# Banded attention with a feed-forward layer, one core: the attention values of twelve pairs move to another PSUM bank and to another place in TensorE's queue

## The chip, the cores and the metric

The kernel runs on one core of a Trainium2 chip. The metric is the time of one execution in device microseconds (us). Before the change, three runs gave 850.41, 850.63 and 853.78 us; the median is 850.63 us.

## What is computed

Queries, keys and values for 8 batches, 8 heads, 576 positions and 64 channels go through attention with a band of 64 positions. The result, 4608 rows of 512, goes through two matrix products with a leaky ReLU between them.

```python
scores = scale * np.matmul(q, k.transpose(0, 1, 3, 2))
mask = (rel >= 0) & (rel < window)          # rel = query - key position, window = 64
attn = softmax of the masked scores
out = np.matmul(attn, v)
x = out as 4608 x 512
h = x @ w_in                                # 512 x 2048
g = np.maximum(0.01 * h, h)
return g @ w_out                            # 2048 x 512
```

## The kernel before

**Attention in pairs.** A block is 64 queries of one batch and all 8 heads. There are 72 blocks, taken two at a time as 36 *pairs* m. For a pair, TensorE writes the scores into two PSUM banks, "s" and "t" (32 matmuls of 64x64 for each bank, 64 in all, L278). VectorE adds the mask (E, L677), GpSimd takes the maximum (P) and the sum (A), VectorE subtracts the maximum (B, L699), ScalarE takes the exponential (X, L703), and TensorE multiplies with the values (V, `values_of`, L751: 32 matmuls that read 128 rows and write 64 columns). ScalarE then copies the values out of PSUM (`take_of`, L758, called the *take* here), and VectorE multiplies them by the reciprocals of the sums (Y, L763).

**The feed-forward layer** comes in stages. Rows 0 to 1535 (pairs 0 to 11, three chunks c of 512 rows) are computed directly. Its first layer makes a unit of 128 channels, `h_f`, in one PSUM bank out of 12 matmuls of 128x512 (`early_first`, L938, two calls of 6 each); its second layer adds each unit to four accumulators, `acc_0` to `acc_3`, with 4 times 3 matmuls (`early_second`, L947). Each factor is held as a high and a low part, hence three products per term. The list `walk` sets which unit follows which: first layer of unit n, then second layer of unit n-2, and so on, 24 matmuls a step. The units' banks alternate between "o" and "h". The unit's eviction is a chain: ScalarE applies the leak in the bank (L952), ScalarE copies the high part to one of two buffers (`gs`, L955; it waits until the second layer of two units before has read that buffer), VectorE makes the low part (L958). The bank is free after that.

All of this runs beside attention for pairs 8 to 19, called *early* in the code (`EARLY = 20`), between about 139 and 309 us of the span. The three later chunk groups use products of a recursive block scheme (m, L1136; y, L1156; z, L1199); pairs 20 to 35 run beside those. The first of them needs the outputs of pairs 12 to 19 as rows of x, by way of DRAM (`x_build`, L912 and L915).

**Where an early pair's values go.** `values_of` takes bank "t" for pairs 8 to 19, one of the two banks of the scores. So a pair's values have to wait until the scores of a pair ahead have been read out of "t", and the scores after that wait for the take.

**What sets the order.** Up to 139 us the order is written out by hand. From there on `op(...)` records each piece of work with its engine, an estimated duration and what it comes after, and `arrange` makes one order for each engine: at every step it takes the piece that can begin first, and of those that can begin then the one with the lowest rank. [...] `next_main` chains the feed-forward matmuls, so these keep their own order and the pieces of attention fall between them. DMAs are issued from ScalarE's (ACT) and SyncE's (SP) queues and, for the stream of weights, from GpSimd's (POOL).

Of the kernel before, what the change touches and what calls it, by code (L numbers as in the profile page):

```python
# [37 lines left out]
PAIRED = 8  # L38
# [5 lines left out]
LAG = 2.0  # L44
ROOMS = 3
OWN = 4
TAKEN = 4
# [57 lines left out]
def band_attention_ffn(ctx: ExitStack, tc: tile.TileContext, qk, vW, vL, w_in, w_out, eye_mask, out, outT):  # L105
# [16 lines left out]

    of_h, of_a = cycle("oh"), cycle("st")

# [300 lines left out]
    def mm1(c, f, part):  # L425

        xh, xl = xs[c]
        ps = bank(next(of_h) if c or f >= half else "h", f"h{c}_{f}_{part.start}")[:, part]
        wh, wl = wi[f]
        terms = [(a, b, k) for k in range(KT) for a, b in ((wh, xh), (wh, xl), (wl, xh))]  # L430
        for n, (a, b, k) in enumerate(terms):
            nc.tensor.matmul(ps, a[:, k, :], b[:, k, part], start=n == 0, stop=n == len(terms) - 1)  # L432
        t = []

        def leak():
            t.append(temps[:, :CH][:, part])
            nc.scalar.activation(t[0], ps, AF.Prelu, alpha=0.01)

        def high():
            t2 = pairs_of_g[next(turns) % 2]  # L440
# [91 lines left out]

    def op(engine, us, fn, *after, rank=1.0, lag=0.12, land=0.0):
        x = dict(engine=engine, us=us, fn=fn, after=[a for a in after if a], rank=rank, lag=lag, land=land, n=len(plan))
        plan.append(x)
# [9 lines left out]
    def arrange():  # L545
# [3 lines left out]
        for x in plan:  # L549
# [3 lines left out]
            if not x["after"]:  # L553
                waiting[x["engine"]].append((0.0, x))
        order, landed = [], [0.0] * LANES

# [3 lines left out]
        while any(waiting.values()):  # L560
# [6 lines left out]
            t, e = best  # L567
            r, x = min((y for y in waiting[e] if begins(*y) <= t), key=lambda y: (y[1]["rank"], y[1]["n"]))
            waiting[e] = [y for y in waiting[e] if y[1] is not x]
# [57 lines left out]

    def next_main(us, fn, *after):
        nonlocal main
        main = op("PE", us, fn, *after, main)  # L630
        return main
# [112 lines left out]
    def values_of(m):  # L744
        ps = bank("t" if early(m) else "oh"[m % 2], f"o{m}")
        for w in range(UNITS):
# [35 lines left out]
    def attend(m, gate):  # L782
# [8 lines left out]
        if m > PAIRED:  # L791
            o["v"] = bulk(partial(load_v, m, nc.scalar), before["X1"], rank=0.3 + late, lag=1.0 + 2 * late, land=6.5 + 2 * late)
        takes = [before["take"], two["take"]] if m == EARLY else []
        if held_back(m - 1) and before:
            takes += [before["B0"], before["B1"]]
        held = held_back(m)
        takes += [before.get("E0"), before.get("E1"), three.get("take"), s_free]
        masks = [op("ACT", ACTS, partial(mask_to, m, j), *takes, rank=0.4 + late) for j in range(2)] if held else takes
        urge = [before["X0"], before["X1"]] if m > EARLY and m % 2 == 0 else []
        o["S"] = op(  # L800
            "PE", 1.0, partial(scores_of, m), o.get("k"), *masks, *urge, before.get("S"),
            rank=0.5 + late, lag=LAG if early(m) else 2 * LAG,
        )
# [19 lines left out]
    def normalise(m):  # L823

        late = 0.0 if early(m) else 0.45
        soon = 0.15 if early(m) and m > 13 else 0.8 + late
        o, before, two, after = at[m], at.get(m - 1, {}), at.get(m - 2, {}), at.get(min(m + 2, EARLY - 1))
# [15 lines left out]
    def finish_of(m, spread, late, soon):  # L843
        o, before, two, after = at[m], at.get(m - 1, {}), at.get(m - 2, {}), at.get(min(m + 2, EARLY - 1))
        mate, ahead = at.get(m ^ 1, {}), at.get(m + 2, {})
        if early(m):
            free = [after["E1"], before.get("take"), o["A0"] if direct(m) else o["I"]]
        else:
            free = [both_free if early(m - 2) else two["Y"]]
            free += [] if m % 2 else [mate["X0"], mate["X1"], ahead.get("S")]  # L850
        o["V"] = op("PE", 1.0, partial(values_of, m), o.get("v"), o["X0"], o["X1"], *free, before.get("V"), rank=0.5 + late, lag=LAG if early(m) else 2 * LAG)
        kept = two.get("kept", [])
        if early(m):
            o["take"] = op("ACT", ACTS, partial(take_of, m), o["V"], *kept, rank=0.5 + late)
        o["Y"] = op("DVE", TWO if early(m) else ONE, partial(product_of, m), *spread, o.get("take"), o["V"], *kept, rank=soon, lag=0.3 + 6 * late)
# [72 lines left out]
    def early_first(n, part):  # L928
        c, f = walk[n]
        xh, xl = xs[c]  # L930
        if part == 0:
            h_of[n] = bank(next(of_h), f"h{c}_{f}")
        ps = h_of[n]
# [45 lines left out]
    def second_step(n):  # L979
        c, f = walk[n]  # L980
        free = evicted[c - 1] if n in opens else [None] * 4
        seconds[n] = [next_main(3 * MM, partial(early_second, n, i), lows[n], free[i], *ready[f]) for i in range(4)]
        if c == 2:
# [8 lines left out]
    for n, (c, f) in enumerate(walk):  # L992
        next_main(6 * MM, partial(early_first, n, 0), lows.get(n - 2), *ready[f], *(x2 if c == 2 else ()))
        first = next_main(6 * MM, partial(early_first, n, 1))
        if n == 0:
# [449 lines left out]
```

## Time and profile before

| | before |
|---|---|
| median of 3 runs | 850.63 us |
| the profiled execution: whole time / its span | 849.76 us / 847.9 us |
| TensorE busy, DVE busy, ACT busy, POOL busy | 839.7, 604.3, 390.1, 383.4 us |
| granted TensorE clock | 1.00 |
| DMA | 226.79 MB, mean 267 GB/s |
| values of the early pairs (L751), first and last take (L758) | 12 takes, 173.9 to 308.9 us |

The profile is one execution of the program. PE is TensorE's matmul row, DVE is VectorE, ACT is ScalarE, POOL is GpSimd. A line of the timeline reads: start, duration, engine, source line, operation, tile written <- tiles read, shape, count, and in square brackets how long the engine stood idle before it and for what. Matmuls overlap, so the duration of a group is not its price; the distance from its start to the next group's start is.

### The profile page before, as it was taken

To read this page: it belongs to the slowest core of one execution; us is meant where nothing else is said; L and a number is where in the kernel's file an instruction comes from. 1 tells how busy PE (TensorE), PEld (TensorE's weight loads), DVE (VectorE), ACT (ScalarE), POOL (GpSimd) and SP (SyncE) were. 2 spreads that over 40 slices of the span, in tenths; PEclk is the share of its full clock that TensorE was granted. 3 is DMA by queue.
4 is the path that set the end of the run, shared out by engine and by line. 5 is a ranking of instruction groups with operands and counts; after the bars stand their busy time and mean duration, and the time that the engine had idled before them with its cause. 6 is when DMAs were issued, how large, how long until landed. Compare 5 with 4: busy or idle time off the path is not lost.

```text
span 847.9 us, 16820 instructions
## 1 busy us (share of the span) xinstructions
PE 839.7 (99%) x6778; PEld 685.6 (81%) x6778; DVE 604.3 (71%) x851; ACT 390.1 (46%) x637; POOL 383.4 (45%) x218
## 2 busy tenths in 40 slices
PE   8999999999999999999999999999999999999998
PEld 5787888888878888888888888888888888888886
DVE  6999885748768778656669956475679855446863
ACT  4666654333433355554554544543354533324431
POOL 5322000878888716776777767855111111111110
PEclk9999999999999999999999999999999999999999
DMA  9874756898899969999999999999998886677682
GB/s 330 268 235 152 252 163 235 265 283 282 272 316 313 318 208 287 303 319 340 334 336 354 361 344 315 363 315 302 260 268 234 236 247 196 199 199 198 193 215 89
DMA packets 143116, 226.79 MB, mean 267 GB/s; under 512 B 15552, under 2 KB 66880, under 8 KB 143040
## 3 DMA queue, kind: packets, MB, share of 16 engines
q0 software_dynamic: 51552, 90.18, 38.3%
q10 hardware_dynamic: 51024, 77.31, 28.5%
q1 hardware_dynamic: 40464, 58.24, 21.1%
q8 instruction: 53, 0.87, 0.4%
q14 instruction: 23, 0.19, 0.1%
HBM read 172.52 MB, written 53.06 MB: 266 GB/s over the span
## 4 chain that ended last, share of the span: by engine, by line
PE 88%; DMA 5%; DVE 5%; ACT 1%; issue 1%; ACTq 0%; SPq 0%; DVEq 0%
PE m L1136 27%; PE z L1199 18%; PE acc L947 11%; PE h L938 11%; PE y L1156 5%; PE h L432 4%; PE acc L468 4%; PE s L278 4%; PE o L751 3%; DMA more_v<-vL 2%; DMA raw<-w_out 1%; DMA late_r<-rows 1%; DMA rows<-late_c 1%; DVE w L242 1%; PE o L368 1%
## 5 line engine op out<-in xcount | busy, mean ns | idle before, releaser
L1136 PE MATMUL m<-pfew,p 128*128 128x512 f32 x720 | 168.7, 390 | 0.0
L1136 PEld LDWEIGHTS m<-pfew,p 128*128 128x128 f32 x720 | 134.6, 188 | 28.3
L1120 POOL DMA_DIRECT2D p<-w_first x42 | 31.7, 755 | 109.0 <-PE m L1136 67.5
L947 PE MATMUL acc<-p,gs 128*128 128x512 f32 x324 | 80.4, 394 | 0.0
L1145 DVE TENSOR_TENSOR p<-m,pxa 128x512 f32<-128x512 f32 x60 | 41.4, 690 | 50.7 <-PE m L1136 48.3
L1145 DVE TENSOR_TENSOR pxa<-m,pxa 128x512 f32<-128x512 f32 x60 | 41.3, 689 | 46.3 <-PE m L1136 45.8
L695 POOL PARTITION_ALL_REDUCE late_o<-late_f x20 | 65.6, 3306 | 16.4 <-ACT late_f L703 9.4
L1148 ACT ACTIVATE p<-p 128x512 f32<-128x512 f32 x60 | 37.8, 631 | 76.3 <-DVE p L1145 76.2
L692 POOL PARTITION_ALL_REDUCE g<-late_f x20 | 36.8, 1872 | 78.7 <-DVE late_f L677 71.3
L1136 PE MATMUL m<-pxb,p 128*128 128x512 f32 x288 | 70.4, 390 | 0.0
L947 PEld LDWEIGHTS acc<-p,gs 128*128 128x128 f32 x324 | 59.9, 188 | 12.8
L695 POOL PARTITION_ALL_REDUCE late_o<-e x18 | 59.8, 3339 | 17.9 <-issue 8.3
L695 POOL PARTITION_ALL_REDUCE late_o<-late_e x18 | 60.1, 3358 | 15.4 <-issue 9.5
L1136 PEld LDWEIGHTS m<-pxb,p 128*128 128x128 f32 x288 | 53.8, 188 | 11.3
L1199 PE MATMUL z<-gs,p 128*128 128x512 f32 x240 | 57.6, 389 | 0.0
L938 PE MATMUL h<-pxa,p 128*128 128x512 f32 x228 | 55.2, 391 | 0.0
L1199 PEld LDWEIGHTS z<-gs,p 128*128 128x128 f32 x240 | 45.0, 188 | 9.4
L1199 PE MATMUL z<-third,p 128*128 128x512 f32 x216 | 51.9, 389 | 0.0
L1199 PE MATMUL z<-pxa,p 128*128 128x512 f32 x216 | 51.9, 389 | 0.0
L1120 POOL DMA_DIRECT2D p<-w_second x28 | 22.7, 811 | 63.9 <-PE z L1199 37.0
L938 PEld LDWEIGHTS h<-pxa,p 128*128 128x128 f32 x228 | 42.6, 188 | 9.0
L1199 PEld LDWEIGHTS z<-third,p 128*128 128x128 f32 x216 | 40.5, 188 | 8.4
(193 smaller groups left out, 1744.4 us busy)
## 6 DMA issues: line engine op xcount, KB each, us to landing
p<-w_first POOLq DMA_DIRECT2D x42, 1024.0 KB, 7.1
p<-w_second POOLq DMA_DIRECT2D x28, 1024.0 KB, 7.7
p<-w_sums POOLq DMA_DIRECT2D x16, 1024.0 KB, 5.6
qk<-qk ACTq DMA_DIRECT2D x26, 512.0 KB, 6.6
pspare<-w_second ACTq DMA_DIRECT2D x16, 512.0 KB, 7.9
w_sums<-pspare ACTq DMA_DIRECT2D x16, 512.0 KB, 7.6
raw<-w_out ACTq DMA_DIRECT2D x15, 512.0 KB, 4.2
raw<-w_in ACTq DMA_DIRECT2D x14, 512.0 KB, 3.8
```

What stands on the lines that cost most here:

```text
L278: nc.tensor.matmul(ps[j][t, c : c + QB], k[i][s, p], q[s, w, p], start=not begun and (not more or (w, p) == (0, 0)), stop=not begun and no ...
L432: nc.tensor.matmul(ps, a[:, k, :], b[:, k, part], start=n == 0, stop=n == len(terms) - 1)
L692: nc.gpsimd.partition_all_reduce(most_of(j), e_of(m)[:, j], P, ReduceOp.max)
L695: nc.gpsimd.partition_all_reduce(sum_of(j), e_of(m)[:, j], P, ReduceOp.add)
L938: nc.tensor.matmul(ps, a[:, k, :], b[:, k], start=i == 0, stop=i == len(terms) - 1)
L947: nc.tensor.matmul(acc[c, i], a[:, i * P : (i + 1) * P], b, start=begin and k == 0, stop=n in ends and k == 2)
L1120: nc.gpsimd.dma_start(to, of, max_dma_last_dim=2048)
L1136: nc.tensor.matmul(tiles[b], w[:, 256 * i + 128 * kt : 256 * i + 128 * kt + 128], x_part(OF_X[k], j, kt), start=begin and c == 0, stop=c = ...
L1145: nc.vector.tensor_tensor(to(), tiles[b], x(), ALU.add)
L1148: nc.scalar.activation(to(), to() if b is None else tiles[b], AF.Prelu, alpha=0.01)
L1156: nc.tensor.matmul(tiles[i], a, b, start=f == 0 and k == 0, stop=f == FT - 1 and k == 2)
L1199: nc.tensor.matmul(tiles[b + i], a, x, start=begin and f == 0 and c == 0, stop=f == half - 1 and c == 2, skip_group_check=not begin,)
```

## The change

Three things are altered. First, the values of pairs 8 to 19 go to that bank of "o" and "h" in which the current first-layer unit does *not* lie (`h_now` remembers the current one), no longer to "t". The unit before the current one lay there, so its low part must have been made, and the next unit must wait for the take: when `arrange` issues the values of a pair, it adds their take to what the next unit's opening comes after. Second, values of pairs 8 to 19 come after the scores of the pair two further on, and scores and values are marked as guests, which `arrange` prefers to place behind a first-layer piece (a host) or behind another guest. Third, some numbers of the planner change: the estimated duration of scores and values goes from 1.0 to 1.15 us, the take's rank from 0.5 to 0.05, and the rank `soon` of an early pair's last steps is 0.15 for all twelve.

```diff
+HOSTS = ("host", None, None, None)
...
+    of_h = cycle("oh")
+    h_now = ["h"]
+
+    def next_h():
+        h_now[0] = next(of_h)
+        return h_now[0]
...
+        def fits(x):
+            return x["place"] != "guest" or last_place in ("host", "guest")
...
-            r, x = min((y for y in waiting[e] if begins(*y) <= t), key=lambda y: (y[1]["rank"], y[1]["n"]))
+            ready_now = [y for y in waiting[e] if begins(*y) <= t]
+            r, x = min([y for y in ready_now if fits(y[1])] or ready_now, key=lambda y: (y[1]["rank"], y[1]["n"]))
+            if e == "PE":
+                last_place = x["place"]
+                if "bank" in x:
+                    for y in [y for y in plan if y.get("opens") and "end" not in y][:1]:
+                        y["after"].append(x["bank"])
+                        missing[y["n"]] += 1
+                        users.setdefault(x["bank"]["n"], []).append(y)
...
     def values_of(m):
-        ps = bank("t" if early(m) else "oh"[m % 2], f"o{m}")
+        ps = bank("oh"[h_now[0] == "o"] if early(m) else "oh"[m % 2], f"o{m}")
...
-        takes = [before["take"], two["take"]] if m == EARLY else []
+        takes = []
...
-        takes += [before.get("E0"), before.get("E1"), three.get("take"), s_free]
+        takes += [before.get("E0"), before.get("E1"), s_free]
...
-            "PE", 1.0, partial(scores_of, m), o.get("k"), *masks, *urge, before.get("S"),
-            rank=0.5 + late, lag=LAG if early(m) else 2 * LAG,
+            "PE", 1.15, partial(scores_of, m), o.get("k"), *masks, *urge, before.get("S"),
+            rank=0.5 + late, lag=LAG if early(m) else 2 * LAG, place="guest" if early(m) and m > PAIRED + 1 else None,
...
-        soon = 0.15 if early(m) and m > 13 else 0.8 + late
+        soon = 0.15 if early(m) else 0.8 + late
...
-            free = [after["E1"], before.get("take"), o["A0"] if direct(m) else o["I"]]
+            free = [ahead["S"] if early(m + 2) else o["A0"] if direct(m) else o["I"], before.get("take"), *two.get("kept", [])]
...
-            o["take"] = op("ACT", ACTS, partial(take_of, m), o["V"], *kept, rank=0.5 + late)
+            o["V"]["bank"] = o["take"] = op("ACT", ACTS, partial(take_of, m), o["V"], *kept, rank=0.05)
...
-        next_main(6 * MM, partial(early_first, n, 0), lows.get(n - 2), *ready[f], *(x2 if c == 2 else ()))
-        first = next_main(6 * MM, partial(early_first, n, 1))
+        next_main(6 * MM, partial(early_first, n, 0), lows.get(n - 2), *ready[f], *(x2 if c == 2 else ()), place="host")["opens"] = True
+        first = next_main(6 * MM, partial(early_first, n, 1), place="host")
```

What that does to the order is shown at three places. Line numbers of the changed kernel are higher than those of the kernel before by 6 to 19 (L751 is L768 there, L938 is L955, L947 is L964).

**TensorE, the values of pair 9** (`o_2119` before, `o_2088` after). Before, they stand between the two halves of first-layer unit `h_9`, away from any scores:

```order
L938 MATMUL h_9_2109<-pxb_853,p_8_90 128x512 x5
L751 MATMUL o_2119<-e,more_v 64x64 [waits DMAHW2_49,DVE_49]
L751 MATMUL o_2119<-e,more_v 64x64 x15
L938 MATMUL h_9_2109<-pxb_853,p_8_90 128x512 x6
L947 MATMUL acc_0_1703<-p_17_1735,gs_81 128x512 [waits Activation_49]
```

After, they follow the last scores of pair 11 (`s_0_2049`, `s_1_2050`):

```order
L284 MATMUL s_0_2049<-qk_84 64x64
L284 MATMUL s_1_2050<-qk_84 64x64
L768 MATMUL o_2088<-e,more_v 64x64 [waits DMAHW2_49,DVE_49]
L768 MATMUL o_2088<-e,more_v 64x64 [waits Activation_49]
L768 MATMUL o_2088<-e,more_v 64x64 x14
L964 MATMUL acc_0_1703<-p_16_1609,gs_82 128x512 [waits Activation_49]
L964 MATMUL acc_0_1703<-p_16_1609,gs_82 128x512 x2
L964 MATMUL acc_1_1708<-p_16_1609,gs_82 128x512 x3
L964 MATMUL acc_2_0_743<-p_16_1609,gs_82 128x512 x3
L964 MATMUL acc_3_0_747<-p_16_1609,gs_82 128x512 x3
L955 MATMUL h_9_2129<-pxb_853,p_8_90 128x512 [waits Activation_49]
```

The values have moved up by 18 of the large matmuls and sit in one visit with the scores; and `h_9` now opens with a wait for ScalarE, the take, where `h_9` before waited for VectorE (the low part of the unit that had lain in that bank). Twelve openings have this wait in the changed order.

**TensorE, the values of pair 18** (`o_3315` before, `o_3383` after). Before, they stand inside a second layer:

```order
L947 MATMUL acc_0_2807<-pfew_85,gs_81 128x512 [waits Activation_49]
L947 MATMUL acc_0_2807<-pfew_85,gs_81 128x512 x2
L751 MATMUL o_3315<-e,v 64x64 [waits DMAHW1_49,Activation_49]
L751 MATMUL o_3315<-e,v 64x64 x15
L947 MATMUL acc_1_2815<-pfew_85,gs_81 128x512 x3
L947 MATMUL acc_2_2820<-pfew_85,gs_81 128x512 x3
L947 MATMUL acc_3_2846<-pfew_85,gs_81 128x512 x3
```

After, they stand in the middle of first-layer unit `h_7`, ahead of the scores of pair 20 (`s_0_3284`):

```order
L955 MATMUL h_7_3372<-pxa_20_2192,p_6_88 128x512 [waits DVE_49]
L955 MATMUL h_7_3372<-pxa_21_2193,p_6_88 128x512
L955 MATMUL h_7_3372<-pxa_20_2192,p_6_88 128x512 x2
L955 MATMUL h_7_3372<-pxa_21_2193,p_6_88 128x512
L955 MATMUL h_7_3372<-pxa_20_2192,p_6_88 128x512
L768 MATMUL o_3383<-e,v 64x64 [waits DMAHW7_49,DVE_49]
L768 MATMUL o_3383<-e,v 64x64 x15
L284 MATMUL s_0_3284<-qk_83,qk_84 64x64 [waits DMAHW4_49]
```

They have moved down by 39 of the large matmuls, and wait for VectorE, since they go to the bank of `h_6`, whose low part VectorE makes last.

**ScalarE, the high part of `h_6`** (`gs_82<-h_6`), on which that low part depends. Before, a piece of the sums (L721) and a DMA stand ahead of the leak, and the high part follows the leak directly:

```order
L721 ACTIVATE late_o_1769<-late_o_1770 64x512 [waits Pool_49]
L1048 DMA p_23_2922<-w_single 128x2x256 [waits DMAHW3_49]
L952 ACTIVATE h_6_3350<-h_6_3350 128x512 [waits PE_49]
L955 CAST gs_82<-h_6_3350 128x512 [waits PE_49,Activation_49]
```

After, a piece of pair 19's sums and a cast of the weights' preparation (`p_24`, which waits for loads and for VectorE) have come between the two:

```order
L969 ACTIVATE h_6_3333<-h_6_3333 128x512 [waits PE_49]
L738 ACTIVATE late_o_1766<-late_o_1766 64x512 [waits Pool_49]
L1076 CAST p_24_2914<-p_24_2914 128x4x256 [waits DMAHW2_49,DMAHW1_49,DVE_49]
L972 CAST gs_82<-h_6_3333 128x512 [waits PE_49,Activation_49]
L929 CAST pxb_3380<-p_25_3055 128x2x256
```

More of the change, by code (lines that the diff above doesn't have):

```diff
@@ L121, in place @@
         return wk.tile([P, 2048 * parts], dtype, tag=f"p{tag}", bufs=1, name=f"p{tag}_{next(tiles_made)}")
-    of_h, of_a = cycle("oh"), cycle("st")
+    of_h = cycle("oh")
[3 more added lines that the diff above has]
+        return h_now[0]
     half = FT // 2
@@ L427, in mm1 @@
         xh, xl = xs[c]
-        ps = bank(next(of_h) if c or f >= half else "h", f"h{c}_{f}_{part.start}")[:, part]
+        ps = bank(next_h() if c or f >= half else "h", f"h{c}_{f}_{part.start}")[:, part]
         wh, wl = wi[f]
@@ L531, in band_attention_ffn, with op @@
     plan = []
-    def op(engine, us, fn, *after, rank=1.0, lag=0.12, land=0.0):
-        x = dict(engine=engine, us=us, fn=fn, after=[a for a in after if a], rank=rank, lag=lag, land=land, n=len(plan))
+    def op(engine, us, fn, *after, rank=1.0, lag=0.12, land=0.0, place=None):
+        x = dict(engine=engine, us=us, fn=fn, after=[a for a in after if a], rank=rank, lag=lag, land=land, n=len(plan), place=place)
         plan.append(x)
@@ L554, in arrange @@
                 waiting[x["engine"]].append((0.0, x))
-        order, landed = [], [0.0] * LANES
+        order, landed, last_place = [], [0.0] * LANES, None
+        def fits(x):
+            return x["place"] != "guest" or last_place in ("host", "guest")
         def begins(ready, x):
@@ L626, in band_attention_ffn, with next_main @@
     main = None
-    def next_main(us, fn, *after):
+    def next_main(us, fn, *after, place=None):
         nonlocal main
-        main = op("PE", us, fn, *after, main)
+        main = op("PE", us, fn, *after, main, place=place)
         return main
@@ L843, in finish_of @@
     def finish_of(m, spread, late, soon):
-        o, before, two, after = at[m], at.get(m - 1, {}), at.get(m - 2, {}), at.get(min(m + 2, EARLY - 1))
+        o, before, two = at[m], at.get(m - 1, {}), at.get(m - 2, {})
         mate, ahead = at.get(m ^ 1, {}), at.get(m + 2, {})
         if early(m):
-            free = [after["E1"], before.get("take"), o["A0"] if direct(m) else o["I"]]
+            free = [ahead["S"] if early(m + 2) else o["A0"] if direct(m) else o["I"], before.get("take"), *two.get("kept", [])]
         else:
@@ L850, in finish_of @@
             free += [] if m % 2 else [mate["X0"], mate["X1"], ahead.get("S")]
-        o["V"] = op("PE", 1.0, partial(values_of, m), o.get("v"), o["X0"], o["X1"], *free, before.get("V"), rank=0.5 + late, lag=LAG if early(m) else 2 * LAG)
+        o["V"] = op("PE", 1.15, partial(values_of, m), o.get("v"), o["X0"], o["X1"], *free, before.get("V"), rank=0.5 + late, lag=LAG if early(m) else 2 * LAG, place="guest" if early(m) else None)
         kept = two.get("kept", [])
         if early(m):
-            o["take"] = op("ACT", ACTS, partial(take_of, m), o["V"], *kept, rank=0.5 + late)
+            o["V"]["bank"] = o["take"] = op("ACT", ACTS, partial(take_of, m), o["V"], *kept, rank=0.05)
         o["Y"] = op("DVE", TWO if early(m) else ONE, partial(product_of, m), *spread, o.get("take"), o["V"], *kept, rank=soon, lag=0.3 + 6 * late)
@@ L931, in early_first @@
         if part == 0:
-            h_of[n] = bank(next(of_h), f"h{c}_{f}")
+            h_of[n] = bank(next_h(), f"h{c}_{f}")
         ps = h_of[n]
@@ L981, in second_step @@
         free = evicted[c - 1] if n in opens else [None] * 4
-        seconds[n] = [next_main(3 * MM, partial(early_second, n, i), lows[n], free[i], *ready[f]) for i in range(4)]
+        seconds[n] = [
+            next_main(3 * MM, partial(early_second, n, i), lows[n], free[i], *ready[f], place=HOSTS[i]) for i in range(4)
+        ]
         if c == 2:
```

## The prediction

> **What bounds the kernel now.** I read the page's busy times and its chain first, then who waits on TensorE.
>
> ```profile
> span 847.9 us, 16820 instructions
> PE 839.7 (99%) x6778; PEld 685.6 (81%) x6778; DVE 604.3 (71%) x851; ACT 390.1 (46%) x637; POOL 383.4 (45%) x218
> ...
> PE 88%; DMA 5%; DVE 5%; ACT 1%; issue 1%; ACTq 0%; SPq 0%; DVEq 0%
> ```
>
> TensorE is busy for 99% of the span and carries 88% of the chain that ends last. A busy PE says little by itself, since matmuls overlap; so I look at its waits, and at the stretch in which pairs 8 to 19 run.
>
> ```profile
> PE idle L504 <- DVE p L515: 1.4, 1, 1.4
> PE s L278 <- ACT late_c L710: 0.9, 1, 0.9
> ```
> ```profile
> 140.00:310.00 170.00, 170.00 (x1747) 137.46 (x1739) 127.22 (x162) 67.50 (x123) 122.32 (x48) 1.00 0.87 283
> ```
>
> The longest wait is at the start (1.4 us), the second is one of 0.9 us. The row is a window of the span (its length, then the busy time of PE, PEld, DVE, ACT and POOL, the granted clock, the DMA engines' busy share and GB/s). From 140 to 310 us PE is busy for 170.00 of 170.00 us, at a granted clock of 1.00. So nothing has to be waited for less: the change can only gain what TensorE spends between matmuls, and loses whatever it makes TensorE wait.
>
> **Term 1, the visits.** I call a run of small matmuls between large ones a visit, and price it from start to start in the timeline.
>
> ```profile
> 192.13 2.88 PE L947 MATMUL acc<-p,gs 128*128 128x512 f32 x12
> 194.85 1.52 PE L938 MATMUL h<-pxb,p 128*128 128x512 f32 x6
> 196.30 1.15 PE L751 MATMUL o<-late_e,v 128*64 128x64 f32 x32
> 197.38 1.66 PE L938 MATMUL h<-pxb,p 128*128 128x512 f32 x6
> 198.87 2.88 PE L947 MATMUL acc<-p,gs 128*128 128x512 f32 x12
> 201.59 1.52 PE L938 MATMUL h<-pxb,p 128*128 128x512 f32 x6
> 203.51 0.69 PE L278 MATMUL s<-qk 64*64 64x64 f32 x34
> 204.14 1.66 PE L938 MATMUL h<-pxb,p 128*128 128x512 f32 x6
> 205.63 2.88 PE L947 MATMUL acc<-p,gs 128*128 128x512 f32 x12
> ```
>
> Twelve undisturbed matmuls take 194.85 - 192.13 = 2.72 us, 0.227 each. The twelve of the next unit, with one pair's values among them, take 198.87 - 194.85 = 4.02: the values cost 1.30 us. With scores they take 205.63 - 201.59 = 4.04: the scores cost 1.32. Apart, the two cost 2.62 us. What they cost together, the trace shows later, where a late pair's values stand behind scores:
>
> ```profile
> 542.84 5.60 PE L1136 MATMUL m<-pfew,p 128*128 128x512 f32 x24
> 548.84 0.69 PE L278 MATMUL s<-qk 64*64 64x64 f32 x34
> 549.46 1.15 PE L751 MATMUL o<-late_f,v 128*64 128x64 f32 x32
> 550.54 1.66 PE L1136 MATMUL m<-pfew,p 128*128 128x512 f32 x6
> 552.04 1.32 PE L1136 MATMUL m<-pxb,p 128*128 128x512 f32 x5
> ```
>
> From 542.84 to 552.04 lie 9.20 us with 30 large matmuls (30 x 0.227 = 6.80); scores and values together cost 2.40. One visit saved is worth 2.62 - 2.40 = 0.22 us. Counted in the two orders, the whole program makes ten visits fewer: of the twelve pairs, nine have their values right behind scores and one right ahead of them, two (pairs 10 and 19) still stand alone; among the pairs from 20 on, one visit is split and another joined. **Term 1 is -10 x 0.22 = -2.2 us.** There is no work beside it to hide it, since PE is full before and after.
>
> [...]
>
> [...]
>
> [...] I take the measured 0.22, which has the step between scores and values in it.
>
> **Term 2, values that wait for the bank.** The bank they take now is free only when the unit before has been evicted: high part, then low part. The high part cannot start before the second layer ahead of the current unit has ended, that is, when the current unit opens. How long the low part then takes:
>
> ```profile
> 194.87 0.59 ACT L955 CAST gs<-h 128x512 fp32r<-128x512 f32 x1 [1.97 <-PE acc L947]
> ```
> ```profile
> 196.83 0.68 DVE L958 TENSOR_TENSOR gs<-h,gs 128x512 fp32r<-128x512 f32 x1
> ```
> ```profile
> 215.10 1.52 PE L938 MATMUL h<-pxb,p 128*128 128x512 f32 x6
> ```
> ```profile
> 215.75 0.69 DVE L958 TENSOR_TENSOR gs<-h,gs 128x512 fp32r<-128x512 f32 x1 [0.38 <-ACT gs L955]
> ```
>
> The unit that opens at 194.85 has the low part ready at 196.83 + 0.68 = 197.51, 2.66 us later; the one at 215.10 at 216.44, 1.34 later. Values behind a full unit and scores start about 2.72 + 1.32 = 4.0 us after the opening: covered. Behind half a unit and scores (pairs 14 and 15) it is about 2.7: just covered. In the middle of a unit without scores ahead (pairs 10, 18, 19) it is 196.30 - 194.85 = 1.45 us: covered in the quick case, 1.2 us short in the slow one. For these three the term lies between 0 and 3 x 1.2 = 3.6. For pair 18 the order puts a cast that waits for VectorE and a piece that waits for GpSimd ahead of the high part, as in the slow case; ahead of the low parts for 10 and 19 nothing new has to be waited for. **I take one slow case, +1.2 us.** Nothing else covers it: PE's queue behind the values is the whole feed-forward layer.
>
> **Term 3, openings that wait for the take.** Behind each pair's values the next unit's opening waits for the take, and behind the opening stand all of PE's matmuls.
>
> ```profile
> 197.50 0.59 ACT L758 COPY late_n<-o 128x512 f32<-128x512 f32 x1
> ```
> ```profile
> 209.81 1.15 PE L751 MATMUL o<-late_f,more_v 128*64 128x64 f32 x32
> ```
> ```profile
> 211.63 0.59 ACT L758 COPY late_n<-o 128x512 f32<-128x512 f32 x1 [2.66 <-DMA qk<-qk]
> ```
> ```profile
> 301.62 1.15 PE L751 MATMUL o<-late_e,more_v 128*64 128x64 f32 x32
> ...
> 302.70 0.96 PE L947 MATMUL acc<-pfew,gs 128*128 128x512 f32 x3
> ```
> ```profile
> 308.89 0.57 ACT L758 COPY late_n<-o 128x512 f32<-128x512 f32 x1
> ```
>
> A prompt take starts 197.50 - 196.30 = 1.20 us after its values and runs 0.59. The next opening comes after 1.08 us (302.70 - 301.62) and twelve second-layer matmuls, so 3.8 us after the values' start at the earliest. The take may be 3.8 - 1.20 - 0.59 = 2.0 us late before PE waits. Pair 11's take is 0.6 us late (211.63 - 209.81 - 1.20), behind a DMA issue: covered. Pair 19's is 308.89 - 301.62 - 1.20 = 6.1 late, but it stood behind other casts with a rank of 0.5; now it goes first whenever it can. In the changed ACT order what stands ahead of a take is a leak, one or two DMA issues or an exponential that is due by then. **I take 0**; the bounds are 0 and 4.1 us (6.1 - 2.0) for each take that is as late as pair 19's.
>
> **Term 4, the next stage.** Values of pairs 18 and 19 come later, and their rows of x feed the first m product.
>
> ```profile
> 329.91 1.23 DVE L915 TENSOR_TENSOR pfew<-p,pfew 128x1024 fp32r<-128x1024 f32 x1 [0.37 <-ACT pfew L912]
> ```
> ```profile
> 339.47 1.52 PE L1136 MATMUL m<-pxb,p 128*128 128x512 f32 x6
> ```
>
> The last piece of x ends at 331.1, and m begins at 339.47: 8.3 us of slack. Pair 19's values move down by 36 large matmuls (8.2 us) and a scores visit (1.32), less term 1, to about 308.9 us; with a prompt take at 310.1 this is 1.2 us later than the late take of before. **0.**
>
> **The sum** against the profiled execution: 849.76 (span 847.9 and 1.9 around it) - 2.2 + 1.2 = 848.8. The median of the runs is 850.63, 0.87 above it; the same difference gives **849.6 us**.
>
> **The rivals.**
>
> *A, late takes (slower).* ACT carries out its queue in turn, so a take behind an instruction that waits for a DMA or for VectorE is late, and past 2.0 us PE's whole queue stands. Two as late as pair 19's give 850.63 - 2.2 + 8.2 = 856.6; one gives 852.5, with the slow low parts more. For it: the 2.66 us that ACT waited at 211.63. Against: five of the twelve takes of before found ACT idle and waiting for them, and now each has the lowest rank.
>
> ```profile
> ACT late_n L758 <- PE o L751: 10.7, 5, 2.5
> ```
>
> It decides from 2.2 us of waits in all. [...]
>
> *B, the DMA takes it back.* Around PE's one late wait the DMA engines are full (a share of 1.19 in this window):
>
> ```profile
> 500.00:510.00 10.00, 10.00 (x67) 8.26 (x60) 6.83 (x11) 3.61 (x7) 4.31 (x3) 1.00 1.19 359
> ```
> ```profile
> 515.72 0.36 PE L278 MATMUL s<-qk,qk 64*64 64x64 f32 x3 [0.88 <-ACT late_c L710]
> ```
>
> If transfers set the pace there, what PE gains before is waited off at that place: 850.6. Against: the transfers are started by PE's progress and so begin earlier too, and PE waits only this once.
>
> *C, no waits at all:* term 2 is 0 and the 0.9 us at 515.72 falls away in the new order: 850.63 - 2.2 - 0.9 = 847.5.
>
> *D, it doesn't do what it says.* The order shows ten joins of twelve, so this is settled but for two.
>
> **How the numbers follow.** Forecast (a gain of up to 2.2): 0.58. A: 0.22. B: 0.12. C: 0.08. The range holds all of the forecast, B, C from its middle price on and A with one late take: 847.4 to 852.6. About 0.5% (4.25 us) is what a measurement of this kernel can tell from no change; below 846.4 nothing in the sum leads, so 0.02 for faster; above 854.9 only A with two late takes does, 0.08; the rest, 0.90, is the same.
>
> **What would show it.** Right, if the PE timeline has nine visits of scores and values between 160 and 310 us with 2.40 us each, and if m begins between 337 and 339.5 us. Term 2 is seen as PE idle ahead of L768 with VectorE (L975) as releaser, term 3 as idle ahead of L955 with ACT L775, B as idle ahead of scores behind 480 us. It is wrong if the joined visits cost as much as two, or if waits of L768 and L955 together exceed 3.5 us.

## The result, and the profile after

| | before | after |
|---|---|---|
| median | 850.72 us (6 runs) | 857.59 us (6 runs, 856.94 to 858.43) |
| ratio to before, 95% interval | | 1.0076 (1.0058 to 1.0093) |
| span of the profiled execution | 847.9 us | 855.2 us |

The change makes the kernel slower by 0.76%; 849.6 had been predicted. First the page of the changed kernel (span, busy times, shares of the chain), then TensorE's waits (total, times, longest):

```profile
span 855.2 us, 16825 instructions
PE 840.5 (98%) x6778; PEld 686.8 (80%) x6778; DVE 600.4 (70%) x851; ACT 390.6 (46%) x637; POOL 384.0 (45%) x218
...
PE 84%; DVE 6%; DMA 5%; issue 2%; ACT 1%; POOL 1%; SPq 0%; ACTq 0%; DVEq 0%; POOLq 0%
```
```profile
PE o L768 <- DVE gs L975: 5.9, 3, 3.7
PE idle L510 <- DVE p L521: 1.4, 1, 1.4
PE m L1155 <- DVE pxa L1164: 0.6, 1, 0.6
PE y L1175 <- issue: 0.6, 1, 0.6
...
PE m L1155 <- ACT p L1167: 0.3, 1, 0.3
...
PE h L955 <- ACT late_n L775: 0.2, 1, 0.2
```

TensorE's share of the chain falls from 88 to 84%. A wait that was not there before leads the list: three pairs' values (L768) wait 5.9 us for low parts (L975). The windows say where, and what comes behind:

```profile
130.00:320.00 190.00, 183.90 (x1884) 150.63 (x1883) 126.54 (x174) 77.11 (x139) 125.74 (x51) 0.99 0.80 267
195.00:200.00 5.00, 1.31 (x22) 0.93 (x22) 4.89 (x4) 0.43 (x1) 4.91 (x3) 0.93 0.50 166
200.00:205.00 5.00, 5.00 (x33) 4.08 (x29) 1.90 (x3) 2.32 (x4) 2.08 (x3) 0.73 0.98 297
```

Between 130 and 320 us, where TensorE had been busy all the time, it is idle for 6.1 us. Most of that is near 197 us, and right behind it the granted clock is 0.73. TensorE's timeline there, and the other two places:

```profile
193.86 1.52 PE L955 MATMUL h<-pxb,p 128*128 128x512 f32 x6
199.07 1.80 PE L768 MATMUL o<-late_e,v 128*64 128x64 f32 x32 [3.69 <-DVE gs L975]
200.80 2.54 PE L955 MATMUL h<-pxb,p 128*128 128x512 f32 x6
203.17 2.89 PE L964 MATMUL acc<-p,gs 128*128 128x512 f32 x12
205.90 2.88 PE L955 MATMUL h<-pxb,p 128*128 128x512 f32 x12
209.19 0.69 PE L284 MATMUL s<-qk 64*64 64x64 f32 x34
209.81 1.15 PE L768 MATMUL o<-late_f,more_v 128*64 128x64 f32 x32
...
213.76 1.52 PE L955 MATMUL h<-pxb,p 128*128 128x512 f32 x6
```
```profile
259.10 1.52 PE L955 MATMUL h<-pxa,pfew 128*128 128x512 f32 x6
...
262.92 1.15 PE L768 MATMUL o<-e,more_v 128*64 128x64 f32 x32 [1.21 <-DVE gs L975]
...
265.50 0.85 PE L964 MATMUL acc<-p,gs 128*128 128x512 f32 x3
```
```profile
306.21 1.52 PE L955 MATMUL h<-pxa,p 128*128 128x512 f32 x6
308.73 1.15 PE L768 MATMUL o<-e,v 128*64 128x64 f32 x32 [1.00 <-DVE gs L975]
...
312.41 0.86 PE L964 MATMUL acc<-p,gs 128*128 128x512 f32 x3
```

Pair 10: from 193.86 to 203.17 lie 9.31 us with 12 large matmuls (2.72), so its values cost 6.59 instead of the 1.30 of a lone visit, **5.3 us too much**: 3.7 of waiting and 1.6 of slow matmuls. A joined visit, that of pair 11: from 205.90 to 213.76 are 7.86 us with 24 large matmuls (5.45), so it costs 2.41. Against that, pair 15 costs 6.40 - 2.72 - 2.41 = 1.3 us too much, and pair 18 (6.20 - 2.72 - 2.41) 1.1. The account: -2.2 for ten joins, +5.3 +1.3 +1.1 is +5.5 of the +7.3 in the spans. It closes where the first m product opens, 5.5 us later than before (339.47):

```profile
345.00 1.38 PE L1155 MATMUL m<-pxb,p 128*128 128x512 f32 x5
```

The rest, 1.8, arises behind that. The waits there (those at L1155 and L1175, 1.5, where before had one of 0.9) are 0.6 of it; the other 1.2 isn't broken down.

Why pair 10 waits, on VectorE's timeline of the changed kernel:

```profile
192.98 0.69 DVE L795 TENSOR_TENSOR pxa<-late_n,pxa 128x512 fp32r<-128x512 f32 x1 [3.88 <-DMA out<-pxa]
193.59 0.68 DVE L716 TENSOR_TENSOR late_f<-late_f,g 128x512 f32<-128x512 f32 x1
...
195.46 2.96 DVE L1079 TENSOR_TENSOR pspare<-pspare 128x1024 fp32r<-128x1024 f32 x1
198.34 0.68 DVE L975 TENSOR_TENSOR gs<-h,gs 128x512 fp32r<-128x512 f32 x1
```

VectorE stands 3.88 us at L795, the low part of pair 8's rows of x (`low_early`). That writes a tile from which chunk 0's results are just being sent to DRAM. Behind it, five instructions take until 198.3, and only then comes h_10's low part, for which pair 10's values wait. In the profile before, the same instruction (L778) stood right ahead of that low part:

```profile
192.06 4.24 DVE L1054 TENSOR_TENSOR pspare<-pspare 128x256 f32<-128x256 f32 x4
196.22 0.68 DVE L778 TENSOR_TENSOR pxa<-late_n,pxa 128x512 fp32r<-128x512 f32 x1
```

It waited for nothing there: the steps L716, L694 and L731 that now follow it had run earlier, and the 4.24 us of L1054 stood right ahead of it. The last of the transfers, issued at 190.25, took 4.9 us to land, so they were through by about 195.1. Both covers are gone in the changed kernel. The rank `soon` (0.8 before for pairs 8 to 13, now 0.15) moved the instruction up past the steps, and the planner's new order has L1054's work (L1073 there) some nine us earlier, from 182.91 on. L1079, which came behind the low part before, stands ahead of it now and takes 2.96 us. The planner knows neither that L795 waits for these transfers nor that values wait for the low part of the unit whose bank they take.

### The profile page after: what moved, and what is told of

Read it like the earlier page. It is cut to its first block, busy times and chain, and to the rows that moved or that the text cites. A ratio compares the mean times of both kernels' runs of the same rounds, so it can differ in the third digit from the quotient of the medians.

```text
span 855.2 us, 16825 instructions
## 1 busy us (share of the span) xinstructions
PE 840.5 (98%) x6778; PEld 686.8 (80%) x6778; DVE 600.4 (70%) x851; ACT 390.6 (46%) x637; POOL 384.0 (45%) x218
## 4 chain that ended last, share of the span: by engine, by line
PE 84%; DVE 6%; DMA 5%; issue 2%; ACT 1%; POOL 1%; SPq 0%; ACTq 0%; DVEq 0%; POOLq 0%
PE m L1155 26%; PE z L1218 18%; PE y L1175 10%; PE acc L964 6%; PE h L955 6%; PE h L438 5%; PE acc L474 5%; PE s L284 3%; PE o L768 3%; DMA x_rows<-late_n 1%; DMA p<-x_rows 1%; PE o L374 1%; POOL late_o L712 1%; DMA raw<-w_out 1%; DMA late_r<-rows 1%
## 5 line engine op out<-in xcount | busy, mean ns | idle before, releaser
L1155 PE MATMUL m<-pfew,p 128*128 128x512 f32 x720 | 168.6, 390 | 0.6 <-DVE pxa L1164 0.6
L1155 PEld LDWEIGHTS m<-pfew,p 128*128 128x128 f32 x720 | 134.8, 188 | 29.1 <-DVE pxa L1164 1.0
L964 PE MATMUL acc<-p,gs 128*128 128x512 f32 x324 | 79.1, 393 | 0.0
L712 POOL PARTITION_ALL_REDUCE late_o<-late_f x20 | 65.6, 3301 | 14.1 <-ACT late_f L720 8.9
L1155 PE MATMUL m<-pxb,p 128*128 128x512 f32 x288 | 71.2, 393 | 0.3 <-ACT p L1167 0.3
L712 POOL PARTITION_ALL_REDUCE late_o<-late_e x18 | 60.2, 3367 | 23.7 <-issue 18.4
L964 PEld LDWEIGHTS acc<-p,gs 128*128 128x128 f32 x324 | 60.1, 188 | 13.1
L712 POOL PARTITION_ALL_REDUCE late_o<-e x18 | 58.7, 3287 | 26.4 <-ACT e L720 12.8
L1155 PEld LDWEIGHTS m<-pxb,p 128*128 128x128 f32 x288 | 53.4, 188 | 12.6 <-ACT p L1167 0.7
L955 PE MATMUL h<-pxa,p 128*128 128x512 f32 x228 | 55.6, 391 | 0.2 <-ACT late_n L775 0.2
L955 PEld LDWEIGHTS h<-pxa,p 128*128 128x128 f32 x228 | 42.5, 188 | 9.5 <-ACT late_n L775 0.6
L975 DVE TENSOR_TENSOR gs<-h,gs 128x512 fp32r<-128x512 f32 x32 | 22.0, 687 | 38.7 <-ACT gs L972 38.7
```

The source lines that it names most:

```text
L712: nc.gpsimd.partition_all_reduce(sum_of(j), e_of(m)[:, j], P, ReduceOp.add)
L955: nc.tensor.matmul(ps, a[:, k, :], b[:, k], start=i == 0, stop=i == len(terms) - 1)
L964: nc.tensor.matmul(acc[c, i], a[:, i * P : (i + 1) * P], b, start=begin and k == 0, stop=n in ends and k == 2)
L1155: nc.tensor.matmul(tiles[b], w[:, 256 * i + 128 * kt : 256 * i + 128 * kt + 128], x_part(OF_X[k], j, kt), start=begin and c == 0, stop=c = ...
```

## The experiments

**Theory R**: the rank brings VectorE to a halt behind transfers, and pair 10's values inherit that. **Rival T**: values in the new bank wait for low parts at any rank. **Rival L**: what is gained early is lost behind 480 us. Each group of runs had its own runs of before, on the same chip (medians 851.0 to 852.3); ratios are to those, from all executions of both, and so not the quotients of the medians. "PE busy" is TensorE's time of the 190 us from 130 to 320, from the same window as above (before: 190.00, after: 183.90).

| run | median | ratio, 95% interval | PE busy |
|---|---|---|---|
| 1 e1_old_rank | 849.72 | 0.9970 (0.9949 to 0.9991) | 189.41 |
| 2 e2_rank_alone | 865.17 | 1.0144 (1.0112 to 1.0177) | 187.22 |
| 3 e3_low_x_behind | 852.07 | 1.0002 (0.9982 to 1.0022) | 187.64 |
| 4 e4_lows_first | 853.01 | 1.0012 (0.9992 to 1.0031) | 188.06 |
| 5 e5_lows_first_again | 850.64 | 0.9983 (0.9960 to 1.0005) | 187.58 |
| 6 e6_late_waits_too | 849.19 | 0.9962 (0.9942 to 0.9981) | 188.21 |
| 7 e7_joins_split | 851.10 | 0.9987 (0.9968 to 1.0005) | 190.00 |
| 8 e8_planner_told | 856.98 | 1.0052 (1.0030 to 1.0073) | 187.50 |
| 9 e9_planner_told_both | 847.55 | 0.9975 (0.9959 to 0.9992) | 190.00 |
| 10 e10_issues_behind | 854.64 | 1.0039 (1.0019 to 1.0060) | 187.58 |
| 11 e11_two_joins_split | 848.74 | 0.9979 (0.9965 to 0.9992) | 190.00 |
| 12 e12_values_held_only | 856.77 | 1.0076 (1.0050 to 1.0103) | 186.56 |

**Runs 1 and 2: the rank.** Each is one line, in the changed kernel and in the kernel before:

```diff
-        soon = 0.15 if early(m) else 0.8 + late
+        soon = 0.15 if early(m) and m > 13 else 0.8 + late
```
```diff
-        soon = 0.15 if early(m) and m > 13 else 0.8 + late
+        soon = 0.15 if early(m) else 0.8 + late
```

> The changed kernel with one line put back: the rank `soon` of pairs 8 to 13 is 0.8 again, so that the low part of pair 8's rows of x (L795) is no longer ahead of the low part of h_10 (L975) in VectorE's queue. The planner then also places the values of pair 10 elsewhere (inside a second layer instead of in the middle of h_11), and splits pairs 15 and 18 from their scores. Theory R (the rank put VectorE behind the output transfers of chunk 0): pair 10's values do not wait, some 5.3 us go, 857.6 - 5.3 = 852.3, give or take 1.5 for the other places that move. Rival T (it is the new bank: values in the middle of a unit wait for the low part at any rank): waits of 1 to 3 us show at each of the pairs that stand alone, 855 or more. Rival L (what is gained before 310 us is lost to transfers behind 480 us): pair 10's wait goes but the time stays at 857 or more.

> The kernel before with only the rank `soon` of the change (0.15 for all of pairs 8 to 19); values stay in bank t. Theory R: VectorE stands some 3 to 4 us at the low part of pair 8's rows of x, with the output transfers as releaser, as in the changed kernel, but no values wait for a low part of the feed-forward layer, so TensorE loses under 1 us there: 850 to 852. If the rank by itself were the price whatever the bank, the time would be 854 or more. Rival T: as before, 850.7, and no such wait of VectorE.

Run 1 came out 2.6 us lower than expected, below before. It isn't a clean test: L795 still stood ahead of h_10's low part and VectorE still stood there (2.83 us), but with less work behind it, and pair 10's values came nine large matmuls later and waited 0.6. So theory R is too narrow as it stands: with the old rank the new order alone, in which the work that had covered the transfers comes earlier, stops VectorE as well. Run 2 missed by 13 us; by its time the other branch came, that the rank costs whatever the bank. Locally it did what theory R says: VectorE stood 4.96 us at that place, and TensorE lost 0.2 there. But the planner's whole order changed, and values in bank t waited elsewhere; the largest loss is one wait for a load of weight sums:

```profile
194.59 1.51 DVE L778 TENSOR_TENSOR pxa<-late_n,pxa 128x512 fp32r<-128x512 f32 x1 [4.96 <-DMA out<-pxa]
```
```profile
PE z L1199 <- DMA p<-w_sums: 7.6, 1, 7.6
```

A change of a rank is no test of one step: it changes all orders. So the next runs moved single instructions by hand in the finished order.

**Run 3: one instruction on VectorE.**

```diff
+    move(at[PAIRED]["kept"][0], lows[10], 1)    # low part of pair 8's rows of x, behind h_10's low part
```

> The changed kernel with one instruction moved in VectorE's queue: the low part of pair 8's rows of x goes behind the low part of h_10, that of L1079 and all else keep their places, and TensorE's order is unchanged. Theory R: the wait of 3.7 us at pair 10's values and TensorE's slow matmuls behind it go, 857.6 - 5.3 = 852.3 (851.5 to 853.2); the waits of pairs 15 and 18 stay at some 1.3 and 1.1 us. Rival T: pair 10 still waits 1 us or more and the time is 854 or above. Rival L: pair 10's wait goes, but waits behind 480 us grow by as much: 856 or more.

VectorE's timeline of run 3 at that place, and its TensorE waits at L768:

```profile
192.93 1.21 DVE L1079 TENSOR_TENSOR pspare<-pspare 128x1024 fp32r<-128x1024 f32 x1
195.04 0.69 DVE L975 TENSOR_TENSOR gs<-h,gs 128x512 fp32r<-128x512 f32 x1 [0.90 <-ACT gs L972]
195.65 1.15 DVE L795 TENSOR_TENSOR pxa<-late_n,pxa 128x512 fp32r<-128x512 f32 x1
```
```profile
PE o L768 <- DVE gs L975: 2.4, 2, 1.7
```

As theory R said: pair 10 waits no more, the slow matmuls are gone (granted clock 1.00 from 195 to 205), and the span is 849.5, that is 5.7 under after (5.5 by the medians), with 5.3 expected. The instruction itself waits no more either, since the transfers have landed by 195.65. Pair 18 waits 1.7 now, though nothing was changed there, and pair 15 0.7. Rivals T and L fall for pair 10: the gain arrives at the end in full, and the waits behind 480 us stay as they were. One thing run 3 doesn't separate: L1079 stayed ahead of the low part, but took 1.21 us here and 2.96 in after. With 1.21 there pair 10 would have waited some 1.9 us instead of 3.69 (an estimate, 3.69 less the difference).

**Runs 4 and 5: the low parts for pairs 15 and 18**, on top of run 3.

```diff
+    for n, k in ((19, 2), (26, 1)):             # run 4
+        move(highs[n], leaks[n], 1)
+        move(lows[n], ahead_of("DVE", lows[n], k), 0)
```
```diff
+    move(highs[26], seconds[24][-1], 1)         # run 5
+    move(lows[26], highs[26], 1)
+    for x in reversed(ahead("ACT", highs[26], 2)):
+        move(x, lows[26], 1)
+    move(lows[19], highs[19], 1)
+    for x in reversed(ahead("DVE", lows[19], 2)):
+        move(x, lows[19], 1)
```

> As the run with the low part of pair 8's rows moved, and for h_12 (the bank that pair 15's values take) and h_6 (pair 18's) the high part is moved on ScalarE directly behind its leak, and the low part on VectorE ahead of the one or two pieces (L1079, Y) that stood before it. Theory R with its second part (pairs 15 and 18 wait for low parts that come late in the queue): 857.6 - 5.3 - 1.3 - 1.1 = 849.9 (849.0 to 851.0), and the waits at L768 fall below 0.5 us in sum. If the two low parts were late for another reason (GpSimd stretching VectorE's work, the new bank's chain itself), the waits stay at 1 us each and the time at 852. Rival L: 852 or more, with the waits behind 480 us grown.

> As the run that moved only the low part of pair 8's rows of x, and in addition the chains that pairs 15 and 18 wait for come first on their engines, each behind what it needs: h_12's low part ahead of the L1079 and the Y that stood before it on VectorE; h_6's high part directly behind its leak on ScalarE, ahead of a piece of the sums (L738, waits for GpSimd) and a cast (L1076), and its low part ahead of that cast's L1079. TensorE's order is unchanged and all that is computed stays. Theory R, second part (these low parts are late because of what stands ahead of them in the two queues): the waits of 0.74 and 1.76 us go, the time is 2.5 us under that run's: TensorE's last matmul starts at 842.8 instead of 845.3, ratio to before about 0.997. Rival T (the new bank makes values wait whatever stands in the queues): both waits stay over 0.7 us. Rival L: they go, but the stages behind 330 us give it back, and the last matmul starts at 845 all the same.

Run 4's edit was mistaken: it put two high parts ahead of the second layers that still had to read the buffer they overwrite, so these layers work on other data and wait for the new ones (1.9 us at L964). It says nothing on the theory. In run 5 pairs 15 and 18 wait no more, but in its profile pair 16 waits 0.3 and pair 17 1.9, and the ratio is 0.9983 where 0.997 was expected. ScalarE's timeline of run 5 (ACTq is its DMA issues), TensorE's wait, and the window behind it:

```profile
283.72 0.58 ACT L969 ACTIVATE h<-h 128x512 f32<-128x512 f32 x1 [7.14 <-DMA qk<-qk]
285.63 0.33 ACTq L1088 DMA_DIRECT2D w_first<-p  x1
286.00 0.63 ACT L720 ACTIVATE e<-e 128x512 f32<-128x512 f32 x1 [1.70 <-DMA p<-x_rows]
286.54 0.57 ACT L972 CAST gs<-h 128x512 fp32r<-128x512 f32 x1
```
```profile
287.88 1.15 PE L768 MATMUL o<-late_f,more_v 128*64 128x64 f32 x32 [1.94 <-DVE gs L975]
```
```profile
289.00:292.50 3.50, 3.50 (x11) 2.76 (x10) 3.46 (x5) 0.59 (x1) 3.50 (x2) 0.53 0.91 217
```

Between the leak (L969) and the high part (L972) ScalarE stood at a DMA issue (L1088) that itself had to wait for another transfer. In run 6, which has the same order up to 320 us, pair 17 didn't wait at all, but pairs 15 (1.1) and 16 did. So these waits change from one execution to the next, and the twelve times of run 5 lie between 846.4 and 856.2. This is **theory R2**: a joined visit leaves the low part only a little time, and ScalarE's and VectorE's queues stand at issues and pieces whose end depends on transfers and on GpSimd.

**Run 6: the late waits**, on top of run 5.

```diff
+    for n in (1667, 1655):                      # a load and a piece of the next rows of x (L932)
+        move(plan[n], plan[1527], 1)            # behind the copy that frees a y bank
+    move(plan[1828], plan[1722], 1)             # a sum of products (L1207) behind two additions (L1164)
```

> As the run with both chains first, with two pieces of VectorE moved behind 480 us: a piece of the next rows of x (L932) goes behind the copy that frees the first y bank (L1178), and a sum of products (L1207), which ran 3.3 us beside GpSimd, goes behind the two additions (L1164) that TensorE waited for. If the late waits of the changed kernel are made by its VectorE order, as theory R has it, the waits of 0.7 and 1.0 us near 480 and 563 go and the time falls by another 1.5 us: last matmul at about 841.3, ratio to before 0.995. If transfers set the pace there (rival L), the last matmul stays at 842.8.

1.45 us under run 5 (849.19), as expected, with intervals that overlap. The waits near 480 and 563 us are gone; one of 0.5 us at L1177 took their place near 500. So most of the late waits come from the changed VectorE order. This version is 0.4% under before, with an interval that stays below 1.

**Run 7: the price of the joins**, on top of run 5.

```diff
+    for m in (8, 9, 11, 12, 13, 14, 15, 16, 17):
+        mine = [y for y in order if y["engine"] == "PE"]
+        behind = mine[next(i for i, y in enumerate(mine) if y is at[m]["V"]) + 1]
+        move(at[m]["V"], behind, 1)
```

> As the run with both chains first, but the values of the nine pairs that stand directly behind scores (8, 9, 11 to 17) go one piece of the feed-forward layer later, three or six large matmuls, into visits of their own; bank and queues are else the same. It prices the joins by themselves. If a joined visit saves 0.20 to 0.22 us (term 1 of the prediction), this is 1.8 to 2.0 us slower than the run with the joins: last matmul at 844.7, ratio to before about 0.999. [...]

The same stretch of TensorE's timeline, split (run 7) and joined (run 3):

```profile
214.46 2.88 PE L955 MATMUL h<-pxb,p 128*128 128x512 f32 x12
...
225.24 1.07 PE L964 MATMUL acc<-p,gs 128*128 128x512 f32 x4
```
```profile
214.44 2.88 PE L955 MATMUL h<-pxb,p 128*128 128x512 f32 x12
...
225.04 1.30 PE L964 MATMUL acc<-p,gs 128*128 128x512 f32 x5
```

10.78 against 10.60 us for the same 36 large matmuls, scores and values: a join is worth 0.18 here, 1.6 for nine. Yet run 7 is only 0.5 us slower than run 5 (851.10 and 850.64, not distinguishable): split, no values wait (PE busy 190.00), and the times lie closer (850.4 to 853.3). By these profiles the joins lose in waits what they save, because they also start the values 0.7 to 1.4 us earlier.

**Runs 8, 9 and 12: tell the planner instead.** Run 8 tells it of the transfers; run 9 also lets values wait for the low part of their bank's unit; run 12 has the second rule alone.

```diff
-            o["kept"] = [op("DVE", TWO, partial(low_early, m), hi, rank=soon)]
+            o["kept"] = [op("DVE", TWO, partial(low_early, m), hi, *sent, rank=soon)]    # runs 8 and 9
...
+            if "bank" in x and not (len(opened) > 1 and lows[len(opened) - 2].get("end", 1e9) + 0.12 <= t):
+                return False                                                              # runs 9 and 12, in fits
```

> The changed kernel, rank included, with one dependency added for the planner: the low part of the early pairs' rows of x comes after the four output transfers of chunk 0, whose staging tile it overwrites. The planner then makes its own order, and places pair 10's values ahead of pair 12's scores and three other pairs elsewhere. Theory R: VectorE no longer stands over 3 us at that low part, TensorE waits nowhere over 2 us between 130 and 320 us, and the time is 850 to 853 (ratio 0.998 to 1.002), like the run that moved that one instruction by hand. If the rank costs by other ways as well, it stays at 855 or more.

> As the run in which the planner knows of the output transfers, and it also holds a pair's values back until, by its own estimates, the low part of the unit in their bank is done. Values move again (pairs 10, 12, 14, 18, 19 by 3 to 21 large matmuls). Theory R2 (the low parts come late because ScalarE and VectorE stand behind issues and pieces that wait for transfers and GpSimd, which the planner's estimates do not know): the waits at L768 fall from 2.4 us but one or two of 0.5 to 2 us stay, and the time is 851 to 856. If the planner's missing dependency were all (theory R alone), no wait at L768 and 849 to 851.

> The other half of the planner's two new rules alone: values are held back until, by its estimates, the low part of the unit in their bank is done, but it does not know of the output transfers, so that the low part of pair 8's rows of x stays ahead of h_10's low part on VectorE as in the changed kernel, and pair 10's values come six large matmuls later than there. Theory R: VectorE still stands 3 to 4 us for the output transfers, and pair 10's values wait some 3.7 - 1.4 = 2.3 us, perhaps with slow matmuls behind it; the other waits at L768 are under 1 us; 849.5 to 853, 2 to 5 us over the run with both rules. If holding the values back were enough by itself, 847 to 849 as with both rules.

Run 8 freed VectorE as expected, but pair 17 waited 1.8 us with slow matmuls behind it, and behind 480 us TensorE waited 2.7 us for a copy (L1179) of ScalarE, which had stood 5.84 us at weight transfers, with 6.8 us of slow clock behind that: 857.0 instead of 850 to 853. Run 9, with both rules, has no wait of TensorE over 0.3 us behind 130 us, and has the lowest median, 847.55; by the ratios, whose intervals overlap, it is level with runs 1, 6 and 11. I had given R2's 851 to 856 for it, and 849 to 851 if the planner's dependencies were all; it came out under both, and the waits that R2 foresaw are not in its profile. Two of its ten times (851.65 and 852.03) lie apart; whether they hold such waits isn't known. Run 12 has the second rule alone:

```profile
192.83 0.69 DVE L801 TENSOR_TENSOR pxa<-late_n,pxa 128x512 fp32r<-128x512 f32 x1 [3.29 <-DMA out<-pxa]
```
```profile
PE o L774 <- DVE gs L981: 3.4, 3, 1.7
PE m L1162 <- DVE pxb L938: 3.4, 1, 3.4
```

VectorE stands at the transfers again (3.29) and pair 10 waits 1.7, some 2 us less than in after since its values come six matmuls later; so far as expected. The 3.4 at the first m were not: pair 19's values came 33 large matmuls later than in after, and its rows of x came late with them. In this order, moreover, pair 20's sum overwrites the reciprocals before pair 19's product has read them: VectorE stood 3.53 us at the product, with that sum as releaser, and pair 19's rows hold other numbers (no work is left out). So run 12 shows that VectorE still stops without the first rule, but its time (856.8, where 849.5 to 853 was expected) is no price of the second.

**Runs 10 and 11: the issues, or the slack**, both on top of run 6.

```diff
+    for m in range(PAIRED, EARLY):              # run 10; n is the unit whose bank pair m's values take
...
+        for x in [y for y in ahead("ACT", highs[n], 4) if y["land"]]:
+            move(x, highs[n], 1)
```
```diff
+    for m in (15, 17):                          # run 11, as in run 7
```

> As the run with the two late places mended too, and on ScalarE every DMA issue that stands within four pieces ahead of a high part whose bank is next taken by values (13 issues, at ten of the twelve pairs) goes directly behind that high part. Nothing moves on TensorE. Theory R2: what made pairs 15, 16 and 17 wait in two profiled runs of one and the same order (1.1 and 0.5 us in one, 1.9 us with slow matmuls behind it in the other) were issues at which ScalarE stood for transfers; they go, the last matmul starts at 842 (843.4 less 1.5), the ratio to before is 0.994 to 0.996, and the twelve or so times lie closer together than 5 us. If the waits come from VectorE or GpSimd instead, 0.5 us or more stays at each of two pairs. If loads that are issued later now come late, new waits for DMA show and the time is 850 or more.

> As the run with the two late places mended too, but the values of pairs 15 and 17, which wait in one profile or the other, go one piece of the feed-forward layer later (three or six large matmuls), out of their scores' visits. It gives up 2 x 0.20 us and gives their low parts 0.7 to 1.4 us more. Theory R2: no wait over 0.6 us at L768, last matmul at 842.6 (843.4 - 1.1 + 0.4), ratio to before 0.994 to 0.997, times within 5 us of each other. If the slack is not what these waits hang on, 1 us or more stays at one of the two.

In the profile of run 10 the waits at L768 are gone, as R2 says, but it is slower, and its times lie 6.9 us apart: the issues now stand ahead of takes, first-layer openings wait 1.9 us for these, and one pair's scores 0.5 us for a load (at 273.2). (The 1.5 at L284 is no part of this: it stands at 22.5 us, where the order is written out by hand; run 4's profile has one of 1.8 there.) The median, 854.64, is 2.4 us over the profiled execution, so the other executions lost more than these lines show. TensorE's waits, and the latest take on ScalarE:

```profile
PE h L955 <- ACT late_n L775: 1.9, 3, 1.6
PE s L284 <- issue: 1.5, 1, 1.5
PE s L284 <- DMA qk<-qk: 0.7, 2, 0.5
```
```profile
289.78 2.82 ACTq L1069 DMA_DIRECT2D p<-w_single  x2
292.64 0.58 ACT L775 COPY late_n<-o 128x512 f32<-128x512 f32 x1 [3.25 <-DMA w_first<-p]
```

In run 11 TensorE is busy for all of the 190 us; ten of its twelve times lie below 851.4, and the profile fell on the slowest (852.2), with waits of 2.5 and 1.5 us behind 490 us. No values wait, as expected. Whether a little more time for two low parts is worth more than their two joins isn't shown: the ratio is 0.9979, run 6's 0.9962, and the intervals overlap.

## Why the prediction was wrong

- **Term 1 (-2.2) was right.** A joined visit costs 2.41 (2.40 predicted), ten are joined. Run 7 prices a join at 0.18 instead of 0.22.
- **Term 2 (+1.2, bounds 0 to 3.6) is the step that failed**; it came to 7.7 (5.3 + 1.3 + 1.1). "Ahead of the low parts for 10 and 19 nothing new has to be waited for" was wrong for 10. The low part of pair 8's rows of x (L795) wasn't new to the queue, but it had lost what had covered the transfers of chunk 0's results: four steps, past which the rank had moved it, and the 4.24 us of L1054, which now came earlier. So the transfers became a wait of 3.88 us, with 4.7 us of work (193.59 to 198.34) between it and h_10's low part. I priced the low part by how long it had taken, not by the queue it now stood in. Run 3 settles that this instruction's place made pair 10 wait; how much of the 3.69 us was L1079's slow 2.96 it leaves open. "Just covered" for pairs 14 and 15 was wrong for 15. For pair 18 the slow case was right, and run 5 bears out its reason; that the size fits so well (1.1 for 1.2) is luck, since in run 3 the same queues gave a wait of 1.7. That slow matmuls follow a long wait was not in the sum (1.6 us).
- **Term 3 (0) was right** within 0.2 us. Run 10 shows its danger: with more issues ahead of the takes it becomes 1.9.
- **Term 4 (0) was right** in the changed kernel: nothing waits at the first m. In run 12 its 8.3 us of slack were used up.
- **The signs.** The nine joined visits came as said. The other two fell out against the prediction: m opens at 345.00 instead of 337 to 339.5, and the waits of L768 and L955 together are 6.1 us, over the 3.5 it had named.
- **The rivals.** A had the right mechanism, a queue that stands at something that waits for a transfer, but put it at the takes, and it was the low parts; that its time (856.6) came near is luck. B falls for pair 10 (run 3). Of C the one half came true, the 0.9 us at 515.72 is gone, but 1.5 us of others came.
- **The chances** were too sure because the bounds of term 2 held only the two durations that the profile before happened to show.

## What to carry to other kernels

When an edit makes the bounding engine wait for a chain on other engines, price the chain by walking the new queue ahead of each link, and ask of every piece that moved up what it will now find unfinished; a piece that waited for nothing before may have been covered by what stood ahead of it. An order made by a planner is only as good as the dependencies that it is told: with two that were missing, the same change is a small gain (0.9975 of before in run 9). And a saving of 0.2 us per visit is soon lost again where it takes 0.7 us of slack from a chain whose queues stand at transfers: joined and split, runs 5 and 7, can't be told apart.

## What the hardware showed

After some waits TensorE runs at half its clock for a while. The granted clock was 0.50 from 199.32 to 202.73 in after, from 289.23 to 292.64 in run 5, from 287.27 to 290.68 and from 485.24 to 492.06 in run 8, from 345.40 to 348.81 in run 12 and from 639.80 to 646.62 in run 2: 3.41 us each time, or twice that. A single stretch cost 1.6 to 1.7 us (after, runs 5 and 8), the double one of run 8 3.3.

The length of the wait alone doesn't decide. 1.9 us brought it in run 5 and 1.8 in run 8, while 1.7 in runs 3 and 12 and even 2.5 in run 11 brought nothing. What fits all of these is a raster, my estimate from the times of the changes: they lie a whole number of pieces of 3.4133 us apart (in after the one at 202.73 and the one at the program's end, 854.68, lie 651.95 us or 191 pieces apart; in run 8 those at 290.68 and 485.24 lie 194.56 us or 57 pieces apart), and what would count is how much of a wait falls into one piece. Below are the piece ahead of run 5's slow stretch, and the two that share run 11's wait of 2.5 us (the first of them begins 87 pieces ahead of the change at 849.47):

```profile
285.81:289.22 3.41, 1.47 (x44) 1.27 (x34) 2.08 (x2) 2.12 (x4) 2.44 (x1) 1.00 0.76 252
```
```profile
552.51:555.92 3.41, 1.69 (x8) 1.07 (x6) 3.15 (x5) 0.79 (x1) 3.41 (x3) 1.00 0.92 283
555.92:559.33 3.41, 2.61 (x11) 2.17 (x12) 3.12 (x4) 3.38 (x8) 1.05 (x2) 1.00 0.91 273
```

TensorE was idle for 1.94 us of run 5's piece, and for 1.72 and 0.80 of run 11's two. In these profiles 1.83 idle in one piece (run 8) is the least that brought the slow clock, and 1.72 the most that did not, so a limit would lie between the two, by estimate. No run was made to test it.

L1079 took 1.21 us in run 3 and 2.96 in after. Sums on GpSimd (L712) ran beside it both times: two from 190.45 to 197.23 in run 3, one from 195.09 to 198.32 in after. Why the one was stretched and the other not wasn't tried.
